# Cutting the last weight load of a decode-attention kernel: pieces of 16, 8, 5, 2 and 1 rows in place of 16, 8, 4, 3 and 1

## The chip, the cores and the metric

The kernel runs on one core of a Trainium2 chip. The metric is the device time of one execution in microseconds (us). A profile of one execution comes with each kernel; its span, from the first to the last instruction, is 1.4 to 2 us shorter than the device time. In the profile PE is the matmul engine (TensorE) and PEld its weight loads, DVE and ACT are the vector and the scalar engine, and SP issues the transfers. A transfer "lands" when its semaphore says that all of its data has arrived. The "granted clock" is the share of full speed at which the throttle let TensorE run. Kernels were compared by their median times and, where ratios are given, by the mean time of one kernel's fast runs over that of the other's fast runs of the same rounds, which is not quite the ratio of the medians quoted beside it.

## The reference, cut to what matters

One query token attends over a cache of 16384 keys in 32 heads of 128, and the concatenated head outputs (4096 numbers) go through an output projection `wo` of 4096 x 512. A small gated MLP (B) is mixed in with a gate `g`.

```python
scores = einsum('bhqd,bhkd->bhqk', q, k_cache) * Dh ** -0.5      # k_cache, v_cache: 1 x 32 x 16384 x 128, bf16
o = einsum('bhqk,bhkd->bhqd', softmax(scores), v_cache)
a = o.transpose(0, 2, 1, 3).reshape(1, 1, 4096) @ wo              # wo: 4096 x 512
return g * a + (1 - g) * b                                        # out: 1 x 1 x 512, bf16
```

The two caches are 268 MB; `wo` is 4.2 MB.

## The kernel before: the parts that matter here

All large loads are issued from one queue (SP). `wo` comes last. It is laid out with 32 rows per partition (a "row" here is 512 numbers in each of the 128 partitions, 128 KB), and it is loaded in five pieces, each with its own semaphore, so that the projection can start on what has arrived.

```python
WO_CUTS = (0, 16, 24, 28, 31, 32)     # pieces of 16, 8, 4, 3 and 1 rows
WIDE = 16
...
for j, (a, b) in enumerate(zip(WO_CUTS[:-1], WO_CUTS[1:])):      # the loads, on SP
    sp.op(lambda e, a=a, b=b: e.dma_start(out=wo[:, a * D:b * D], in_=wo_src[:, a * D:b * D]),
          wait=[user[wo_at - 3]] if a == 0 else (), inc=(ld_o[j], 16))
```

The first 16 rows are multiplied four at a time into four column groups ("wide", L106 in the profile), and ACT copies the sums out. The other 16 rows are added to the output one by one (L716). Each of them takes two matmuls of 256 columns, for the two halves of the output. The first row of a piece waits for the piece. The wide half's sums are added, in fp32, after row 23.

```python
def add(lhsT, rhs, wait, mark=False):
    for s in range(NC):                                          # NC = 2, DQ = 256
        ok = pe.op(lambda e, s=s: e.matmul(a_ps[32*s:32*s+1, 0:DQ], lhsT=lhsT,
                   rhs=rhs[:, s*DQ:(s+1)*DQ], ...), wait=wait if s == 0 else (), ...)
...
for j, (a, b) in enumerate(zip(WO_CUTS[:-1], WO_CUTS[1:])):
    for k in range(max(a, WIDE), b):
        y_ok = add(o2[:, k:k+1], wo[:, k*D:(k+1)*D], [(ld_o[j], 16)] if k == a else (), k == H - 1)
    if b == 24:
        add(ones_f[:, 0:1], d_sb[:, :], [w_ok])                  # the wide half, fp32
# then DVE and ACT each cast 256 sums to bf16 (L731), and one DMA writes 512 numbers out (L735)
```

The softmax here doesn't subtract the row's maximum and nothing guards it: scores larger than these inputs give would overflow.

## Time and profile before

| | before |
|---|---|
| median of the first three runs (range) | 652.59 us (651.76 to 652.7) |
| span of the profiled run | 650.2 us |
| load queue's share of 16 DMA engines | 99.6% |
| from the end of the last wo landing to the end of the span | 2.0 us |

Three lines of the page of the kernel before: the DMA row of the 40 slices (9 means 90% or more busy), the load queue (packets, MB, share of the 16 engines' span) and the bytes moved.

```profile
DMA  9999999999999999999999999999999999999998
...
q1 hardware_dynamic: 6194, 279.58, 99.6%
...
HBM read 279.58 MB, written 0.00 MB: 430 GB/s over the span
```

The DMA engines are over 90% busy in every slice but the last. So hardly anything can be gained by sparing an engine work, unless it shortens what comes after the last bytes. The end of the chain of waits of the kernel before (start in us, duration in us, what) says the same:

```profile
...
619.02 28.88 DMA bufs<-in_A_wo_dram
647.89 0.04 issue
647.94 0.65 PE ps_all L716 x8
648.58 0.02 issue
648.61 0.41 DVE res L731
```

A transfer of the fourth piece ends at 647.89, and eight matmuls follow back to back, that is three rows of the fourth piece and the last row. The timeline of the kernel before shows these microseconds by engine. Its columns are the start in us, the time in us, engine, line, operation, what it writes and reads, the count and, in brackets, how long the engine was idle before it and what ended that.

```profile
646.80 0.60 PE L716 MATMUL ps_all<-d_sb,const-float32-1.0 128*1 128x256 f32 x4
647.02 0.52 PEld L716 LDWEIGHTS ps_all<-bufs,o 128*1 128x1 bf16 x8
647.23 1.31 PE L716 MATMUL ps_all<-bufs,o 128*1 128x256 bf16 x16
647.94 0.38 PEld L716 LDWEIGHTS ps_all<-bufs,o 128*1 128x1 bf16 x8 [0.40 <-DMA bufs<-in_A_wo_dram]
648.61 0.36 ACT L731 CAST res<-ps_all 1x256 bf16<-1x256 f32 x1 [1.93 <-PE ps_all L716]
648.61 0.41 DVE L731 CAST res<-ps_all 1x256 bf16<-1x256 f32 x1 [6.07 <-PE ps_all L716]
649.06 0.32 SPq L735 DMA_DIRECT2D out_dram<-res  x1
```

There is one wait for a transfer, of 0.40 us, before the fourth piece, and none before the last row.

The landings are not printed as times. They are read in the trace from each transfer's semaphore, as the time of its sixteenth and last step (one step for each DMA engine). In the kernel before the pieces of 16, 8, 4, 3 and 1 rows land at 643.13, 645.62, 646.91, 647.89 and 648.19 us.

### The profile page before, as it was taken

To read this page: it belongs to the slowest core of one execution; us is meant where nothing else is said; L and a number is where in the kernel's file an instruction comes from. 1 tells how busy PE (TensorE), PEld (TensorE's weight loads), DVE (VectorE), ACT (ScalarE), POOL (GpSimd) and SP (SyncE) were. 2 spreads that over 40 slices of the span, in tenths; PEclk is the share of its full clock that TensorE was granted. 3 is DMA by queue.
4 is the path that set the end of the run, shared out by engine and by line. 5 is a ranking of instruction groups with operands and counts; after the bars stand their busy time and mean duration, and the time that the engine had idled before them with its cause. 6 is when DMAs were issued, how large, how long until landed. Compare 5 with 4: busy or idle time off the path is not lost. (4 is left out here: it accounts for less than half of the span.)

```text
span 650.2 us, 7753 instructions
## 1 busy us (share of the span) xinstructions
PE 424.3 (65%) x2474; PEld 47.0 (7%) x1312; DVE 335.8 (52%) x159; ACT 45.8 (7%) x112; POOL 2.2 (0%) x10
## 2 busy tenths in 40 slices
PE   0646687847477574857757486584748857478678
PEld 0000000000101000010000101000010100001022
DVE  3457839256380835628165370835628174465600
ACT  2210000100001000010100001000000100001011
POOL 1000000000000000000000000000000000000000
PEclk9959798958889796888969679796977969698979
DMA  9999999999999999999999999999999999999998
GB/s 384 463 419 452 452 395 443 452 443 395 452 452 395 443 452 448 391 452 452 403 435 452 448 391 452 452 431 407 452 452 395 443 452 439 399 435 468 392 428 342
DMA packets 6203, 279.60 MB, mean 430 GB/s; under 512 B 695, under 2 KB 826, under 8 KB 1210
## 3 DMA queue, kind: packets, MB, share of 16 engines
q1 hardware_dynamic: 6194, 279.58, 99.6%
q8 instruction: 1, 0.02, 0.0%
q10 hardware_dynamic: 8, 0.00, 0.0%
HBM read 279.58 MB, written 0.00 MB: 430 GB/s over the span
## 5 line engine op out<-in xcount | busy, mean ns | idle before, releaser
L579 DVE TENSOR_TENSOR bufs<-bufs,qb x64 | 281.4, 4418 | 170.8 <-DVEq L86 170.8
L91 PE MATMUL ps_all<-bufs,ident 128*128 x960 | 258.8, 423 | 0.0
L496 PE MATMUL ps_all<-bufs,ident 128*128 x64 | 28.6, 446 | 154.2 <-PEq L86 153.9
L106 PE MATMUL ps_all<-bufs,p_t 128*8 x1024 | 82.5, 396 | 30.1 <-PEq L86 20.1
L564 DVE TENSOR_REDUCE s_sb<-ps_all 128x64 f32<-128x512 f32 x64 | 44.0, 687 | 93.1 <-DVEq L86 93.1
L91 PE MATMUL ps_all<-zero,ident 128*8 128x512 bf16 (+2 forms) x167 | 59.5, 388 | 0.0
L592 ACT ACTIVATE p_t<-s_sb 64x256 f32 (+1 forms) x32 | 13.3, 415 | 433.1 <-ACTq L86 432.7
L496 PEld LDWEIGHTS ps_all<-bufs,ident 128*128 128x128 bf16 x64 | 6.3, 99 | 365.6 <-issue 365.6
L106 PEld LDWEIGHTS ps_all<-bufs,p_t 128*8 x1024 | 19.4, 83 | 163.1 <-issue 161.6
L531 PE MATMUL ps_all<-pick,d_sb 128*128 128x2 f32 x128 | 17.0, 255 | 16.5 <-PEq L86 16.5
L531 PEld LDWEIGHTS ps_all<-pick,d_sb 128*128 128x128 f32 x128 | 15.7, 193 | 34.7 <-issue 34.7
L601 ACT COPY d_sb<-ps_all 128x512 f32<-128x512 f32 x16 | 9.4, 586 | 105.4 <-ACTq L86 105.4
L606 ACT CAST ps_all<-zero 128x512 f32<-128x512 bf16 x15 | 8.8, 589 | 1.7
L666 DVE RECIPROCAL rl<-ps_all 128x32 f32<-128x32 f32 x1 | 0.4, 357 | 12.2 <-PE ps_all L552 12.2
L381 DVE TENSOR_TENSOR bufs<-ps_all,ident 128x896 f32<-128x896 f32 x2 | 2.1, 1086 | 8.6 <-PE ps_all L91 8.6
L669 DVE TENSOR_TENSOR o_sb<-ps_all,rl 128x32 bf16<-128x32 f32 x1 | 0.2, 191 | 11.5 <-PE ps_all L531 11.5
L592 ACT ACTIVATION_READ_ACCUMULATOR p_t<-s_sb (+1 forms) x32 | 5.9, 185 | 0.0
L321 PE MATMUL ps_all<-xgw,const-float32-1.0 1*128 1x3 f32 x2 | 0.6, 360 | 8.0 <-DVE xgw L317 8.0
L91 PE MATMUL ps_all<-bufs,xb 128*128 x12 | 5.0, 552 | 0.0
L106 PE MATMUL ps_all<-bufs,u 128*1 x14 | 2.6, 372 | 3.1 <-ACT ps_all L427 2.4
L345 PE MATMUL ps_all<-bufs,xb 128*128 x4 | 2.3, 574 | 3.3 <-DMA bufs<-in_B_w_in_dram 3.3
L106 PE MATMUL ps_all<-bufs,xb 128*64 x32 | 3.6, 380 | 0.0
(76 smaller groups left out, 40.2 us busy)
## 6 DMA issues: line engine op xcount, KB each, us to landing
bufs<-in_A_k_cache_dram SPq DMA_DIRECT2D x2, 4096.0 KB, 36.2
bufs<-in_A_v_cache_dram SPq DMA_DIRECT2D x1, 5120.0 KB, 34.5
bufs<-in_A_wq_dram SPq DMA_DIRECT2D x1, 4096.0 KB, 12.3
bufs<-in_A_v_cache_dram SPq DMA_DIRECT2D x1, 2048.0 KB, 39.0
bufs<-in_A_wo_dram SPq DMA_DIRECT2D x1, 2048.0 KB, 25.4
bufs<-in_B_w_in_dram SPq DMA_DIRECT2D x1, 1792.0 KB, 15.5
bufs<-in_A_v_cache_dram SPq DMA_DIRECT2D x1, 1024.0 KB, 41.0
bufs<-in_A_wo_dram SPq DMA_DIRECT2D x1, 1024.0 KB, 27.6
```

Source lines behind the costliest of these rows:

```text
L91: ins = eng.matmul(out, lhsT=lhsT, rhs=rhs, **flags).ins
L106: ins = eng.matmul(bank[0:m, 0:n], lhsT=lhsT, rhs=rhs, **flags).ins
L321: g_ok = pe.op(lambda e: e.matmul(g_ps, lhsT=ones_f[0:1, :], rhs=xgw[:, :], start=True, stop=True), wait=[xgw_ok], mark=True)
L345: if n else matmul_on(nc, e, lambda: e.matmul(args[0], lhsT=args[1], rhs=args[2], **flags), [at, (xa, 0)]))
L381: dve.op(lambda e, h=h, zh=zh: e.tensor_tensor(out=zm[:, 2 * h * ZB:2 * (h + 1) * ZB].rearrange("p (b m k) -> p b m k", b=2, k=FhC), in0=z ...
L496: matmul_on(nc, e, lambda: e.matmul(s3, lhsT=ident[:, :], rhs=k3[:, :, 0:W], start=True, **flags), [(kw, 0)])
L531: ins = e.matmul(o2, lhsT=d_sb[:, r * Dh:(r + 1) * Dh], rhs=pick[:, r * 2:(r + 1) * 2], start=False, stop=False, skip_group_check=True)
L564: return e.tensor_reduce(out=s_sb[:, c * QK:(c + 1) * QK], in_=s_ps[c % 2].rearrange("p (j w) -> p j w", w=W), axis=AX.X, op=ALU.add)
L579: e.tensor_tensor(out=k3, in0=k3, in1=qi, op=ALU.mult).then_inc(mul_s, 1)
L592: e.activation(out=p_t[rows, bass.ds(at, NG * 8)].rearrange("p (t c) -> p t c", c=8)[:, :, 4 * s:4 * s + 4], in_=s_sb[rows, :].rearrange(" ...
L601: return e.copy(out=d_sb[:, :], in_=d_ps)
L606: e.copy(out=d_ps, in_=zero[:, :]).then_inc(drn_s, 1)
```

## The change

The intent is to take work off PE late in the tail. One of the three rows that must be multiplied after the fourth piece has landed moves to the third piece, which lands earlier.

```diff
-WO_CUTS = (0, 16, 24, 28, 31, 32)
+WO_CUTS = (0, 16, 24, 29, 31, 32)
```

The built programs differ only in where the third transfer ends and the fourth begins, and in which row of PE waits for the fourth piece.

## The prediction

> **What bounds the kernel now.** The transfers. The page gives the DMA engines 9 tenths or more in 39 of 40 slices, and the load queue 99.6% of 16 engines' span (279.58 MB). The chain that ended last is almost all "DMA bufs<-in_A_wo_dram"; that piece of 28.88 us ends at 647.89 us of a 650.2 us span. So the change can act only on about the last 2.3 us.
>
> **The tail before, from the trace.** The five wo pieces (16, 8, 4, 3, 1 rows) land at 643.13, 645.62, 646.91, 647.89 and 648.19 us. In the timeline PE adds one row each 0.108 us (two 256-column matmuls). It finishes the fp32 addition of the wide half and starts the 4-row piece at 647.23 us, 0.3 us after that piece landed. Its last row starts at 647.56; then the weight-load side waits 0.40 us for DMA. The 3-row piece starts at 647.94, 0.05 us after its landing, its rows at 647.94, 648.05 and 648.15. The last row's weights load at 648.23, 0.04 us after the last landing, and its matmuls start at 648.26. The casts start at 648.61, the output DMA at 649.06.
>
> **What the change does.** Instructions and their order are the same on PE, DVE, ACT and POOL; only the third and fourth wo transfers differ (2560 and 1024 columns in place of 2048 and 1536), and one row's two matmuls wait for the earlier piece. Bytes are equal. Tail packets take about 161 ns for 4096 B, 126 for 3072 and 46 for 1024. I estimate from these 199 ns for 5120 B and 86 for 2048: 285 against 287 ns per partition, 8 packets per engine, so the last landing moves under 0.02 us.
>
> The 5-row piece should land one row later: 0.98 us for three rows between the landings before, so 646.91 + 0.33 = 647.24, about when PE gets free (647.23). Its rows run from about 647.28 to 647.82. The 2-row piece lands at about 647.89 and runs from 647.94 to 648.15. The last row then waits only for its own landing at 648.19 and starts at about 648.235 in place of 648.26. So the gain is about 0.03 us: moving a row saves PE's queue 0.108 us, but only 0.03 lies above the floor that the last landing sets.
>
> The Trainium skill ("DMA: Bandwidth & Descriptors", section "Anatomy of one DMA") says that a transfer's completion comes after its last byte is confirmed written. The trace agrees: the last 1024 B packet ends at 647.74 and the piece lands at 648.19. That 0.45 us is untouched.
>
> **Prediction.** 652.5 us, 8 times in 10 within 651.3 to 653.5; the three runs before differ by 0.94 us, thirty times the gain. Faster by over 2%: 0.003; within 2%: 0.994; slower: 0.003.
>
> **What would show each step.** Landings near 647.24, 647.89 and 648.19, as distances from each other; PE's wait for the fourth piece shrunk from 0.40 us to about 0.1; a new wait below 0.1 us before the last row; the chain of waits ending in the last wo piece; last landing to casts falling from 0.42 to about 0.39 us.
>
> **What would make it wrong.** A 5-row piece landing so late that PE still works on it when the last piece lands; a lower granted clock in the tail (it was 1.00), under which PE's queue would set the end and the gain be 0.1 us; another chip's transfer speed, in which the change has no part.

## The result, and the profile after

| | before | after |
|---|---|---|
| median of 6 runs (range) | 651.88 us (651.63 to 652.7) | 652.0 us (651.68 to 652.78) |
| ratio of the fast runs, after over before | | 1.0, 95% interval 0.9987 to 1.0013 |
| profiled run: last wo landing to start of casts | 0.418 us | 0.384 us |

The time did not move. In the profile of the kernel after, the timeline of the same stretch reads:

```profile
646.97 0.60 PE L716 MATMUL ps_all<-d_sb,const-float32-1.0 128*1 128x256 f32 x4
647.42 0.42 PEld L716 LDWEIGHTS ps_all<-bufs,o 128*1 128x1 bf16 x10 [0.35 <-DMA bufs<-in_A_wo_dram]
647.42 1.25 PE L716 MATMUL ps_all<-bufs,o 128*1 128x256 bf16 x16
648.08 0.09 PEld L716 LDWEIGHTS ps_all<-bufs,o 128*1 128x1 bf16 x4 [0.24 <-DMA bufs<-in_A_wo_dram]
648.40 0.08 PEld L716 LDWEIGHTS ps_all<-bufs,o 128*1 128x1 bf16 x2 [0.23 <-DMA bufs<-in_A_wo_dram]
648.74 0.36 ACT L731 CAST res<-ps_all 1x256 bf16<-1x256 f32 x1 [1.89 <-PE ps_all L716]
648.74 0.41 DVE L731 CAST res<-ps_all 1x256 bf16<-1x256 f32 x1 [6.07 <-PE ps_all L716]
649.19 0.32 SPq L735 DMA_DIRECT2D out_dram<-res  x1
```

The landings are at 643.31, 645.79, 647.38, 648.03 and 648.36 us. Every piece of the queue is now waited for: five rows (10 weight loads), then two, then one, each with its own wait. The last row starts at 648.40, 0.04 us after its landing. Before, it started 0.07 us after it, because the three rows of the fourth piece were still in the queue. So the change did what it was meant to do, and in these two profiles it was worth 0.03 us.

The landings are 0.1 to 0.2 us later on the clock of this run, which is no doing of the change: the first piece, which the change leaves alone, is later by 0.18 us too. (Most of that is one late DMA engine: in this profile the sixteenth step of the first piece comes 0.25 us after the fifteenth, in the profile of before 0.10 us.) The distance from the first to the last landing is 5.06 us before and 5.05 us after.

The chain of waits of the kernel after is no witness. This is all of it but the bare "issue" pieces:

```profile
...
645.83 0.39 PE ps_all L106 x4
646.21 0.16 PE ps_all L91
646.37 2.34 PE ps_all L716 x35
...
648.74 0.41 DVE res L731
```

It follows PE back without a break, since the modelled end of each matmul lies behind the start of the next, and it never meets a transfer. Read alone, it would say that the end is bound by PE more than before. The two 0.2 us waits of the weight loads above say the contrary.

### The profile page after: what moved, and what is told of

It reads as the page before. It is cut to its first block, busy times and chain, and to the rows that moved or that the text cites. A ratio compares the mean times of both kernels' runs of the same rounds, so it can differ in the third digit from the quotient of the medians.

```text
span 650.3 us, 7754 instructions
## 1 busy us (share of the span) xinstructions
PE 433.5 (67%) x2475; PEld 45.9 (7%) x1312; DVE 336.3 (52%) x159; ACT 45.8 (7%) x112; POOL 2.1 (0%) x10
## 3 DMA queue, kind: packets, MB, share of 16 engines
q1 hardware_dynamic: 6194, 279.58, 99.6%
## 5 line engine op out<-in xcount | busy, mean ns | idle before, releaser
L91 PE MATMUL ps_all<-bufs,ident 128*128 x960 | 269.1, 439 | 0.0
L496 PE MATMUL ps_all<-bufs,ident 128*128 x64 | 29.0, 453 | 146.4 <-PEq L86 146.4
L106 PE MATMUL ps_all<-bufs,p_t 128*8 x1024 | 80.3, 388 | 28.9 <-PEq L86 18.3
```

Of the source, the lines that this page charges most:

```text
L91: ins = eng.matmul(out, lhsT=lhsT, rhs=rhs, **flags).ins
L106: ins = eng.matmul(bank[0:m, 0:n], lhsT=lhsT, rhs=rhs, **flags).ins
L496: matmul_on(nc, e, lambda: e.matmul(s3, lhsT=ident[:, :], rhs=k3[:, :, 0:W], start=True, **flags), [(kw, 0)])
```

## The experiments

The theory to be tested, the "floor" theory: the last row starts at the later of two times. One is its own landing plus 0.04 us. The other is the end of the rows queued ahead of it, 0.108 us each. In the kernel before the two differed by 0.03 us, so nothing that PE is spared can bring more. The rivals: the last landing alone sets the end in both kernels, and the 0.03 us is scatter of the profile; PE's queue still sets the end after the change; or the other piece sizes cost the transfers what PE gained. Twelve runs were made, of ten kernels: the two above and eight others. They ran on three chips (12, 6 and 8 on record), so times are compared only with runs of the kernel before in the same rounds.

### Two more profiles of each kernel

No edit; the four runs are one look each.

> A second profile of the kernel before. Floor theory (the last row starts at the later of its own landing plus 0.04 us and the end of the rows queued ahead of it on PE): last wo landing to casts 0.42 us again, because the 3-row fourth piece and the distance of the last two landings (0.30 us) are the same. Rival (the 0.03 us between the first two profiles is scatter of the profile): anything from 0.36 to 0.45 us. Both: time within 0.5 us of the other runs.

> A second profile of the kernel after. Floor theory: last wo landing to casts 0.38 us again. Rival (scatter): anything from 0.36 to 0.45 us, no order against the kernel before. First wo landing to last wo landing 5.05 us in both kernels if the change leaves the transfers alone; a rival in which the 5-row or the 2-row piece costs the transfers time would show over 5.1 us here and 5.05 in the kernel before.

> A third profile of the kernel before: last wo landing to casts 0.42 us if the value belongs to the kernel.

> A third profile of the kernel after: last wo landing to casts 0.38 us if the value belongs to the kernel.

All distances in us, read from the trace:

| profile | first to last landing | 4th to 5th landing | last landing to last row | last landing to casts | time of the run |
|---|---|---|---|---|---|
| before | 5.06 | 0.29 | 0.074 | 0.418 | 651.64 |
| before_again | 5.03 | 0.28 | 0.085 | 0.429 | 652.38 |
| before_third | 5.15 | 0.47 | 0.045 | 0.385 | 652.83 |
| after | 5.05 | 0.32 | 0.043 | 0.384 | 651.76 |
| after_again | 5.06 | 0.30 | 0.044 | 0.385 | 651.59 |
| after_third | 5.05 | 0.30 | 0.043 | 0.384 | 651.74 |

The kernel after gives 0.384 or 0.385 us three times: it stands on the floor. The kernel before gives 0.418 and 0.429, and once, against what was expected, 0.385. In that third profile the last landing came 0.47 us after the fourth in place of 0.28 or 0.29, and so late that the three rows of the fourth piece were done. That is the floor theory's own condition, but it was not foreseen: the gain of the change depends on how far apart the last two landings happen to be, and here it would have been nothing. The transfers cost the same in both kernels (5.03 to 5.06 us, third profile of before aside). The time of before_again is no witness: 652.38 us goes with a span of 650.4 us, 0.2 us over that of the first profile, so most of its excess lies outside the span.

That third profile is also 1.2 us longer than the first (651.4 against 650.2 us of span). The trace shows where most of it comes from. These are steps of the last three wo transfers' semaphores, in us (read from the trace, not a view of the profile). Of the sixteen, the first, the fourteenth, the fifteenth and the sixteenth are given.

```
before         4-row piece: 646.29 ... 646.72 646.81 646.91   3-row: 647.28 ... 647.70 647.81 647.89   1-row: 647.62 ... 648.01 648.10 648.19
before_third   4-row piece: 646.37 ... 646.94 647.10 648.02   3-row: 647.35 ... 647.93 648.08 648.93   1-row: 647.71 ... 648.23 648.37 649.40
```

The last of the sixteen steps, that is one DMA engine, is about 0.9 us behind the other fifteen. Going back through the trace, the distance between the fifteenth and the sixteenth step is 0.01 us for the load that lands at 96.2 us, 0.91 us for the one at 116.7 us, and 0.86 to 1.03 us for every load from there to the end. The Trainium skill says (page "DMA: Bandwidth & Descriptors", section "Why a DMA increments its semaphore by 16 and not by 1") that a transfer's engines finish independently and that only the full count of 16 means all data landed. This trace agrees, with its 0.9 us: fifteen engines wait for nobody, the kernel waits for the sixteenth. The packets narrow down what set it back: of the 64 KB packets, whose median is 2.42 us, seven took over 2.55 us, all of which started between 95.2 and 97.6 us, and the longest took 3.49 us, which is 1.07 us too long. Why these were slow is open. In this run it is most of the 1.2 us, and thirty times what the change can bring.

### The last row's transfer taken away

These two kernels do not load row 31; its two matmuls use row 30's weights. The result is wrong. (It passed the comparison with the reference all the same, so that comparison could not have told.)

```diff
-    for j, (a, b) in enumerate(zip(WO_CUTS[:-1], WO_CUTS[1:])):
+    for j, (a, b) in enumerate(zip(WO_CUTS[:-2], WO_CUTS[1:-1])):
         sp.op(... dma_start ...)
...
-            y_ok = add(o2[:, k:k + 1], wo[:, k * D:(k + 1) * D],
-                       [(ld_o[j], 16)] if k == a else (), k == H - 1)
+            y_ok = add(o2[:, k:k + 1], wo[:, min(k, 30) * D:(min(k, 30) + 1) * D],
+                       [(ld_o[j], 16)] if k == a and k < 31 else (), k == H - 1)
```

> Wrong result on purpose: the kernel before without the transfer of row 31; its two matmuls use row 30's weights. Floor theory: in the kernel before the last landing hardly binds (0.03 us), so the fourth landing to the casts stays what it was, 0.71 us (0.05 + 3 x 0.108 + 0.343). Rival (the last landing alone sets the end): it would fall by the 0.3 us between the last two landings, to about 0.4 us.

> Wrong result on purpose: the kernel after without the transfer of row 31. Floor theory: here the last landing does bind, so the fourth landing to the casts falls from 0.71 us to 0.05 + 2 x 0.108 + 0.343 = 0.61 us. Rival (PE's queue binds in the kernel after too): it stays 0.71 us.

| us | fourth landing to casts, with row 31's transfer | without it |
|---|---|---|
| pieces of before | 0.712, 0.712 (0.851 in the profile with the late engine) | 0.712 |
| pieces of after | 0.706, 0.684, 0.684 | 0.603 |

The first row's values are of before, before_again and before_third, the second's of after, after_again and after_third. In the kernel before, taking away the last transfer changed nothing: the last row was waiting for PE's queue, not for its data. In the kernel after, it took 0.08 to 0.10 us off: there the last row had been waiting for its data. The limit had moved from the queue to the landing. The weight loads of the two runs show it in the timeline, first without row 31 and with the pieces of before, then with the pieces of after:

```profile
647.83 0.31 PEld L716 LDWEIGHTS ps_all<-bufs,o 128*1 128x1 bf16 x8 [0.34 <-DMA bufs<-in_A_wo_dram]
648.50 0.36 ACT L731 CAST res<-ps_all 1x256 bf16<-1x256 f32 x1 [1.88 <-PE ps_all L716]
```

```profile
647.75 0.20 PEld L716 LDWEIGHTS ps_all<-bufs,o 128*1 128x1 bf16 x6 [0.20 <-DMA bufs<-in_A_wo_dram]
648.32 0.36 ACT L731 CAST res<-ps_all 1x256 bf16<-1x256 f32 x1 [1.76 <-PE ps_all L716]
```

Eight weight loads (four rows) against six (three rows) follow the fourth landing without a wait. The casts come 0.67 us against 0.57 us after those loads start, which is the one row of difference.

### More rows behind a late landing

```diff
-WO_CUTS = (0, 16, 24, 28, 31, 32)
+WO_CUTS = (0, 16, 24, 25, 31, 32)      # cut25: the change turned the other way
+WO_CUTS = (0, 16, 24, 32)              # last8: no small pieces
+WO_CUTS = (0, 16, 17, 31, 32)          # fourth14, with "if b == 24" made "if b == 17"
+WO_CUTS = (0, 16, 24, 30, 31, 32)      # cut30: the change carried one row further
```

> Pieces of 16, 8, 1, 6 and 1 rows, the change turned the other way. Floor theory: casts at the fourth landing + 0.05 + 6 x 0.108 + 0.343 = 1.04 us, that is 0.72 us after the last landing; time 0.3 us over the kernel before, likely within its scatter. Rival (the cut between third and fourth piece has no effect at any place): 0.38 to 0.42 us after the last landing.

> Pieces of 16, 8 and 8 rows: no small last pieces at all. Floor theory: casts at the last landing + 0.04 + 7 x 0.108 + 0.343 = 1.14 us, 0.7 us slower than the kernel before (ratio 1.0011), less up to 0.1 us if two transfers fewer let the last bytes land earlier. Rival (transfers alone): no change or 0.1 us faster.

> Pieces of 16, 1, 14 and 1 rows, with the fp32 addition after row 16: the fourth piece is far too large for the 0.3 us between the last two landings. Floor theory: casts at the fourth landing + 0.05 + 14 x 0.108 + 0.343 = 1.9 us, about 1.6 us after the last landing in place of 0.42, so 1.2 us slower than the kernel before (ratio 1.0018). Rival (the time is set by the transfers alone, rows on PE are free whatever their order): no change, 0.0 us.

| kernel | last landing to casts: expected, measured (us) | median time (us) and range | kernel before, same rounds | ratio, 95% interval |
|---|---|---|---|---|
| cut25 | 0.72, 0.752 | 651.95 (651.89 to 652.1) | 652.13 (651.6 to 652.51) | 0.9999, 0.9983 to 1.0014 |
| last8 | 1.14, 1.149 | 652.27 (652.23 to 653.13) | 652.13 (651.6 to 652.51) | 1.0006, 0.9992 to 1.0019 |
| fourth14 | 1.6, 1.537 | 652.79 (652.62 to 652.93) | 652.13 (651.6 to 652.51) | 1.0011, 0.9997 to 1.0024 |

The distances behind the last landing fall where the count of rows puts them, to within 0.07 us. That is a strong test of the floor theory, for the expected values span 0.7 to 1.6 us. (The 0.06 us of fourth14 comes of its last two landings, which were 0.38 us apart and not 0.3.) In the time, even fourteen rows in the wrong piece barely show: 1.2, 0.7 and 0.3 us more were expected for fourth14, last8 and cut25, and the medians differ from before by +0.66, +0.14 and -0.18 us. All five runs of fourth14 lie above all nine runs of before, but the interval of the ratio still holds 1. The spans of the same runs, which leave out the 1.4 to 2 us around the span, show more: their medians are 651.4, 650.8 and 650.55 us against 650.3 us of before (to 0.1 us), so +1.1, +0.5 and +0.25 us. They are in the order and near the size of what was expected. (The granted clock was 1.00 from 646 us on in all three; in cut25, as in the two runs drop31_before and four_groups, it had been lower before that.) Two lines of the timeline of fourth14 show the thirty weight loads (15 rows) that follow its fourth piece's landing, and the late casts:

```profile
647.84 1.51 PEld L716 LDWEIGHTS ps_all<-bufs,o 128*1 128x1 bf16 x30 [1.03 <-DMA bufs<-in_A_wo_dram]
649.71 0.36 ACT L731 CAST res<-ps_all 1x256 bf16<-1x256 f32 x1 [3.04 <-PE ps_all L716]
```

> Pieces of 16, 8, 6, 1 and 1 rows: the change carried one row further. Floor theory: the 6-row third piece lands 0.65 us later than the 4-row one and its six rows end on PE about 0.05 us after the last landing, so the row of the fourth piece and the last row queue behind them: casts 0.50 to 0.55 us after the last landing, worse than 0.38 after. Rival (the smaller the fourth piece the better): 0.38 us.

Measured for cut30, in one look: casts 1.427 us after the last landing. Neither theory gave that, and the run says nothing of the cut. Stretches of the profile of cut30 show the reason. The columns are the stretch, its length, busy us and count of each engine, granted TensorE clock, DMA share and GB/s. The last line is of the kernel before, for comparison.

```profile
640.00:644.00 4.00, 3.52 (x18) 1.62 (x16) 0.60 (x3) 0.41 (x1) 0.00 (x0) 0.60 0.96 406
644.00:647.00 3.00, 3.00 (x29) 1.18 (x26) 0.00 (x0) 0.00 (x0) 0.00 (x0) 0.50 0.98 397
647.00:648.00 1.00, 0.95 (x15) 0.41 (x8) 0.00 (x0) 0.44 (x1) 0.00 (x0) 0.70 0.47 153
648.00:649.00 1.00, 0.80 (x12) 0.49 (x14) 0.00 (x0) 0.15 (x1) 0.00 (x0) 1.00 0.00 0
...
644.00:646.00 2.00, 1.55 (x17) 0.44 (x16) 0.00 (x0) 0.00 (x0) 0.00 (x0) 1.00 0.97 394
```

The granted clock was 0.50 from 644 to 647 us, where it was 1.00 in the profiles of before and after. A row took 0.21 us in place of 0.108 (from row to row in this trace). The wide half and the rows behind it ran late, ACT's copy of the wide half started at 647.56, and the fp32 addition, which waits for it, came at 648.20:

```profile
648.20 0.09 PEld L716 LDWEIGHTS ps_all<-d_sb,const-float32-1.0 128*1 128x1 f32 x4 [0.54 <-ACT d_sb L711]
648.42 0.96 PEld L716 LDWEIGHTS ps_all<-bufs,o 128*1 128x1 bf16 x16
```

Eight rows (16 weight loads) then had to follow, after nearly all data had landed. Whether a cut at row 30 is worse at a full clock stays open. What the run did show is the case that the prediction had named as its risk: under a low clock in the tail PE's queue sets the end, here by a whole microsecond. It shows this for the cuts of cut30; neither the kernel before nor the one after was caught with a low clock in the tail.

### Do the transfers bound the rest?

```diff
+        if kind == "k" and i == 8:
+            cuts = (0, KP // 2)        # half of one pair's keys; wrong result on purpose
```

> Wrong result on purpose: the ninth pair's K load brings half of its rows, 2.1 MB less of 279.6. If the transfers bound the whole kernel at 27.06 B/ns on each of 16 engines (65536 B in 2422 ns), the time falls by 2.1 MB / 433 GB/s = 4.8 us, and the tail's landings keep their distances. Rival (PE, DVE or the buffer waits carry part of the time in mid-kernel): less than 4 us.

The expectation has an error of arithmetic. A pair's K load is 8.4 MB, so half of it is 4.2 MB, not 2.1 MB; the page of this run shows the 4.2 MB:

```profile
HBM read 275.38 MB, written 0.00 MB: 429 GB/s over the span
```

With that size the theory's rule gives 4.2 MB / 433 GB/s = 9.7 us. Measured: 643.6 us against 652.13 us, ratio 0.9868 (0.9853 to 0.9884), so 8.5 us less by the medians. The expectation as written, 4.8 us, is missed; the theory gets back most, not all, of what the corrected sum promises. The profiled run shows where the rest went. In the first profile of before, full loads land 19.34 to 19.36 us apart in mid-kernel. Here three stretches take longer: 0.60 us more for the load that lands at 116.1 us, long before the halved one; 0.94 us more for the load behind the halved one; and 0.36 us more for two loads that land at 417.2 and 436.7 us. The first and the third go along with slow packets (17 of the 64 KB packets took over 2.55 us there, where the median is 2.42; before has none such, before_again 18), and why those are slow is open. The second is the test's own doing. The load behind the halved one is a V load, which must wait until ACT has freed its buffer. In the issues by SP, first of before and then of drop_mid, it comes at nearly the same time in both:

```profile
316.68 0.33 SPq L638 DMA_DIRECT2D bufs<-in_A_v_cache_dram  x1
...
317.85 0.33 SPq L640 DMA_DIRECT2D bufs<-in_A_v_cache_dram  x1
```

In before the K load ahead of it lands only at 328.40 us. In drop_mid the halved one lands at 319.27 us: the engines end its packets between 317.69 and 318.80 us, and each stood idle for about 1.0 us before its first packet of the V load. So the rival that the expectation named, a buffer wait, was at work in the test, because the halved load used up the queue's lead; in before the queue does not run dry there. Less data in mid-kernel is less time, at close to the engines' rate, but this single form of the test does not settle it to better than an eighth.

### A try at the floor itself

After the change, what is left behind the last landing is one row's matmuls, the casts and the output DMA. This kernel has the change's cuts and shortens the first two: four column groups of 128 outputs in place of two of 256.

```diff
-NC = 2
+NC = 4
...
-    res = sb("res", [1, D], BF16)
+    res = sb("res", [P, DQ], BF16)
...
+    for q, h in ((dve, 0), (act, 64)):     # each cast covers two groups, 32 partitions apart
+        ok = q.op(lambda e, h=h, copy=(q is act): (e.copy if copy else e.tensor_copy)(
+            out=res[h:h + 33, :], in_=a_ps[h:h + 33, 0:DQ]), wait=[y_ok], mark=True)
...
-    sp.op(... dma_start(out=out.rearrange("a b d -> (a b) d"), in_=res[:, :]) ...)
+    sp.op(... dma_start(out=out.rearrange("a b (s d) -> (a b s) d", s=NC), in_=res[0:P:32, :]) ...)
```

> A try at what is left after the last landing: the sums of the output lie in four column groups of 128 in place of two of 256, each row takes four matmuls of 128 columns, each cast covers two groups at once, and the output leaves from four partitions. If matmuls of different column groups overlap as the pairs do now, a row takes about 0.06 us in place of 0.108, and the last row's matmul and the casts of half as many columns get shorter: estimate 0.05 us on PE and 0.13 us on the casts, so the output DMA is issued about 0.6 us after the last landing in place of 0.83 (after). Time 0.2 us less, within the scatter; the output DMA's four short rows may give it back.

Its timeline ends so:

```profile
648.61 0.09 PEld L716 LDWEIGHTS ps_all<-bufs,o 128*1 128x1 bf16 x4 [0.21 <-DMA bufs<-in_A_wo_dram]
648.92 0.26 ACT L729 CAST res<-ps_all 33x128 bf16<-33x128 f32 x1 [1.85 <-PE ps_all L716]
648.92 0.28 DVE L729 CAST res<-ps_all 33x128 bf16<-33x128 f32 x1 [5.47 <-PE ps_all L716]
649.27 0.63 SPq L732 DMA_DIRECT2D out_dram<-res  x1
```

The casts start 0.347 us after the last landing (0.384 after the change) and take 0.28 us in place of 0.41, and the output DMA starts 0.70 us after the last landing in place of 0.84: a gain of 0.14 us, less than the 0.23 us expected. But the output DMA now takes 0.63 us to issue in place of 0.32, and from its start to the end of the span are 1.67 us in place of 1.15. That costs 0.5 us. Median time 652.37 us (651.9 to 652.45) against 651.78 us (651.54 to 652.23) of the kernel before, ratio 1.0006 (0.9992 to 1.0019): no gain is shown. The median span is 650.5 us against 650.2 us, which fits the sum of the two, 0.4 us more. The four packets of 256 B take 15 to 16 ns each in this trace, so the data is not what takes long; the instruction's 0.63 us is twice the other's, and its first packet starts 0.60 us after that in place of 0.43. The same sums gathered into one partition for the output were not tried.

No version with the right result was measurably faster than the two kernels.

## Why the prediction was right, point by point

- **"The transfers" bound the kernel.** The load queue is at 99.6% in both profiles, and half a K load less took 8.5 us off. Held, with the reservation made there.
- **"The last landing moves under 0.02 us."** The distance from the first to the last wo landing is 5.06 and 5.03 us before (5.15 with the late engine), 5.05, 5.06 and 5.05 after. Held, as far as it can be seen: two profiles of before alone differ by 0.03 us. The estimated packets were good: for 5120 B, 199 ns estimated and 200.5 measured; for 2048 B, 86 estimated and 84 measured (medians of the 128 packets of a size in each profile of after).
- **The landing of the 5-row piece.** The prediction put it 647.24 − 645.62 = 1.62 us behind the second piece; it was 1.58 us three times. The fourth was expected 0.65 us later and came 0.66, 0.69 and 0.68 us later. Held.
- **"The last row then waits only for its own landing."** It starts 0.043 to 0.044 us after it in all three profiles. The two runs without row 31's transfer show that this was not so before and is so after. Held.
- **"The gain is about 0.03 us", and "last landing to casts falling from 0.42 to about 0.39".** 0.418 and 0.429 before, 0.384 and 0.385 after. Held, with a condition that the prediction lacked: in the profile with the late engine the kernel before had 0.385 too, and the gain was nil.
- **The steps that failed.** "The chain of waits ending in the last wo piece" did not come: the chain ran through PE, because modelled matmul ends hide a wait of PE. And the two waits in the weight loads were mis-sized: "about 0.1" for the fourth piece was 0.24 us, and "below 0.1 us" for the last row was 0.23 us. The prediction had counted PE's free slots (a row each 0.108 us). The profile counts from the end of the last weight load, which runs ahead of the matmuls. On PE's slots, the two waits in the first profile after are 0.12 and 0.11 us (next slot at 647.96 and 648.29, starts at 648.08 and 648.40).
- **The time.** 652.0 us against 652.5 predicted, because the kernel before itself came out at 651.88 us in six runs where three had given 652.59. Nothing of that is due to the change. The time is no test of the mechanism either: the change could act on 2.3 us of 650, so "within 2%" would have held with any gain; only the distances test it.
- **The skill's part of it.** The prediction took from the Trainium skill (page "DMA: Bandwidth & Descriptors", section "Anatomy of one DMA") that a landing comes after its last byte is confirmed. That section describes DMAs issued by GpSimd; these loads are issued by SP, and their trace shows the same order. From the end of the last packet to the landing were 0.445 us before (0.435 in before_again) and 0.42, 0.43 and 0.47 us after: about the same, as predicted.

## What to carry to other kernels

When the last loads are cut into pieces, the compute that waits for piece n needs only to be over by the time piece n+1 lands; sparing more brings nothing, and the last landing is a floor. Work out both times (here 0.108 us per row against 0.3 us between landings) before moving a cut; with 0.03 us between them, no cut can be seen in a time that scatters by 0.9 us. Where a larger effect drowns in the times, compare the spans: they showed 1.1 us for fourth14 where the medians of the times showed 0.66. Look at waits of weight loads, not at the chain through matmuls with modelled ends, and at the clock of the tail before reading a single profile.

## What the Trainium skill lacked or had wrong

- Page "DMA: Bandwidth & Descriptors": it says that engines finish independently, but has no case of one among loads issued by SP that falls behind once and then stays behind for the rest of a kernel. In one run one engine was about 0.9 us late from 116.7 us to the end at 649.4 us, through more than thirty loads, and its span was 1.2 us longer than that of the first profile. In drop_mid the sixteenth step was 0.57 to 0.60 us behind the fifteenth from 116.1 us until the queue ran dry, and 0.02 us for the next load.
- The same page, section "Anatomy of one DMA", gives about 2.0 us of fixed cost for DMAs issued by GpSimd, most of it the confirmation of the write, and has no figure for loads into SBUF issued by SP. Here, for such loads, the last packet's end to the semaphore's last step was 0.42 to 0.54 us in all profiles but two (0.59 us in before_third, with the late engine, and 0.64 us in cut30).
- The same page has no figure for a small output DMA spread over partitions: 512 numbers from one partition took 0.32 us to issue and 1.15 us to the end of the span, from four partitions 0.63 and 1.67 us.
- Page "Perfetto Trace Analysis", section "Tensor Engine Instruction": it says that the profiled end of a matmul is estimated and not observed. It does not say what follows for a chain of waits: 0.23 and 0.24 us of waiting were seen in the weight loads of the kernel after, and its chain ran through them as PE work.
